# One stretch of tiled matmuls per batch over all eight PSUM banks, with four output banks and earlier loads of x

## The chip, the cores and the metric

The kernel runs on one core of a Trainium2 chip. The metric is the device time of one execution, in microseconds (us); lower is better. A kernel is run several times and the median is quoted. All runs quoted here count as undisturbed: none was more than 1.5% above the fastest run of the same kernel. Engines: PE is TensorE (matmuls), PEld its weight loads, DVE is VectorE, ACT is ScalarE, POOL is GpSimd, SP issues most of the DMAs (41 of the 53 that the page of the kernel before lists).

## The reference

The work is two layers. A cross-attention between x (8 batches, 8 heads, 512 positions, 64 wide) and a small state (32 positions per head) gives `xread` (512 rows) and `sread` (32 rows) per batch. A feed-forward layer with SiLU follows.

```
scores = 0.125 * x @ state^T;  a  = softmax(scores);   xread = a  @ state
scores2 = 0.125 * state @ x^T; a2 = softmax(scores2);  sread = a2 @ x
h = concat(xread, sread) laid out as (8 * 544 rows, 512)
out = silu(h @ w_in) @ w_out        # w_in 512 x 2048, w_out 2048 x 512
```

The kernel never forms `xread`. It multiplies state by `w_in` first (`W1 = state @ w_in`, per batch), and then `g = silu(a @ W1)`. `sread` is kept for a short ninth batch at the end.

## The kernel before: the parts that matter

Batch 0 and the start of batch 1 run in a hand-made prologue. Then come phases. **Phase k computes the output of batch k** (`g2`: four output tiles `tt` of 16 matmuls each) and, between these matmuls, does the attention and the `g` matmuls of batch k+1 (`att_tail`) and starts batch k+2 (`att_head`). The program order is fixed by hand: each engine gets its instructions in the order in which these functions are called. `fill[step]` holds what is called after output matmul number `step` (0 to 63).

The program uses eight PSUM banks, called o0, o1, w0, w1, h0, h1, a0, a1. A matmul that overwrites a bank has to wait until the bank's last contents were copied out ("evicted").

```python
def w1_m(b, j, bks):                 # a quarter of W1: 8 small matmuls, 64 x 32 tiles of the array
    for kt in range(KT):
        for half in range(2):
            nc.tensor.matmul(bank[bks[half]][ds(32 * kt, 32), :],
                sbd[ds(64 * half, 64), b, kt, half, :],
                w_in_sb[ds(64 * half, 64), kt, ds(512 * j, 512)], ...,
                tile_position=(64 * half, 32 * kt))

def w1_e(b, j, bks, engs):           # evict both banks of a quarter
    for half in range(2):
        cp(engs[half], W1[b % 2][:, half, ds(512 * j, 512)], bank[bks[half]][:])

def sread_m(b, bk): ...              # 32 small matmuls, 128 x 32 tiles
def norm_s(b, kt=0, n=4): ...        # VectorE: sums of exp, then reciprocal (n of 4 head groups)
def norm_m(b, eng, kt=0, n=4): ...   # VectorE or POOL: multiply by the reciprocal
def a_Td(b): ...                     # DMA that transposes the result into aT, which g1 reads

def g2(b, tt, ft, bk): ...           # one output matmul, 128 x 512
def o_e(b, tt, bk, eng="dve"): ...   # evict an output tile (VectorE copy), DMA it out

WP = (("w0", "w1"), ("h0", "h1"))
def W1p(b, i):                       # half of W1
    for j in range(2): w1_m(b, 2 * i + j, WP[j])
    for j in range(2): w1_e(b, 2 * i + j, WP[j], DD if j == 0 else ("act", "act"))

def phase(k, fill):
    for tt in range(4):
        bk = ("o0", "o1")[tt % 2]    # two output banks
        for ft in range(16):
            g2(k, tt, ft, bk)
            for f in fill.get(16 * tt + ft, ()): f()
        o_e(k, tt, bk)

def att_tail(fill, b, s, a0, sg, dg):
    add(fill, s, L(exs, b), L(W1p, b, 0), L(norm_s, b))          # exs: ScalarE, exp of the scores
    add(fill, s, L(norm_m, b, "dve", 0, 2), L(norm_m, b, "pool", 2, 2))
    add(fill, s, L(nc.scalar.preload_act_table, SILU))
    add(fill, s + 14, L(W1p, b, 1), L(sread_m, b, "a1"), L(sread_n, b, "a1"))
    # ... a_Td at s, sread_t at a0 + 2, sixteen g1 at sg + dg * i

for k in range(2, 7):                # the five steady phases
    fill = {}
    if k + 2 < B: load_x(k + 2, nc.sync)
    att_tail(fill, k + 1, 0, 24, 35, 1.8)
    # ... cast_xu(k + 2) at 0, att_head(k + 2) at 34 and 56
    phase(k, fill)
```

The softmax here doesn't subtract the row's maximum and nothing guards it: scores larger than these inputs give would overflow.

## Time and profile before

| | before |
|---|---|
| median time, us | 222.31 (3 runs; 222.56 with the later rounds) |
| span in the profile, us | 220.9 |
| PE busy | 210.1 us, 95% |
| granted PE clock | 1.00 in every stretch of the phases |
| a steady phase (from one phase's last output copy to the next one's) | 23.15 us (119.20 to 142.35) |

From the profile's page of the kernel before: PE's busy time, and the shares of the chain of work that ended last.

```profile
PE 210.1 (95%) x1632; PEld 103.9 (47%) x1659; DVE 83.5 (38%) x162; ACT 133.0 (60%) x219; POOL 40.8 (18%) x78
...
PE 84%; DMA 7%; ACT 3%; issue 3%; POOL 1%; DVE 1%; ACTq 0%
```

PE bounds the kernel. The next busiest engine, ScalarE, has 60%.

PE's timeline at the start of a steady phase, kernel before. Columns: start, length in us, engine, source line, operation, output and inputs, sizes, count, and in brackets any idle time ahead of it with what ended it.

```profile
96.16 0.41 PE L251 MATMUL ps_w<-w_in_sb,sbd 64*32 64x512 bf16 x8
96.39 0.56 PE L251 MATMUL ps_h<-w_in_sb,sbd 64*32 64x512 bf16 x8
97.11 2.97 PE L296 MATMUL ps_o<-w_out_sb,g 128*128 128x512 bf16 x13 [0.16 <-issue]
100.01 0.41 PE L251 MATMUL ps_w<-w_in_sb,sbd 64*32 64x512 bf16 x8
100.24 0.40 PE L251 MATMUL ps_h<-w_in_sb,sbd 64*32 64x512 bf16 x8
100.57 0.43 PE L218 MATMUL ps_a<-x_n,en 128*32 128x65 bf16 x32
101.15 2.54 PE L296 MATMUL ps_o<-w_out_sb,g 128*128 128x512 bf16 x11 [0.16 <-issue]
```

Two stretches of tiled matmuls (L251 is W1, L218 is sread) interrupt the output matmuls (L296). Full matmuls start 0.2155 us apart. The profile draws one as 0.38 us long, since they overlap. The record of the first matmul after each switch is missing, so one slot has to be added back when the gaps are measured. The two stretches then cost about 0.82 and 1.02 us.

VectorE's timeline in the next steady phase, kernel before:

```profile
119.20 0.69 DVE L79 COPY o_sb<-ps_o 128x512 f32<-128x512 f32 x1 [7.11 <-PE ps_o L296]
119.81 1.28 DVE L79 CAST W<-ps_w 128x512 bf16<-128x512 f32 x2
122.07 1.22 DVE L181 TENSOR_REDUCE rs<-en 128x32 f32<-128x1024 bf16 x1 [0.98 <-ACT en L171]
123.32 0.35 DVE L182 RECIPROCAL rs<-rs 128x32 f32<-128x32 f32 x1
123.71 0.69 DVE L186 TENSOR_TENSOR an<-en,rs 128x512 bf16<-128x512 bf16 x1
124.32 1.28 DVE L79 CAST W<-ps_w 128x512 bf16<-128x512 f32 x2
...
125.92 0.68 DVE L79 COPY o_sb<-ps_o 128x512 f32<-128x512 f32 x1
...
142.35 0.69 DVE L79 COPY o_sb<-ps_o 128x512 f32<-128x512 f32 x1 [7.11 <-PE ps_o L296]
```

The normalisation (L181, L182, L186) cannot start before exp is done on ScalarE, and the copy of the phase's first output tile (125.92) comes behind it. PE does not mind here: that bank, o0, is next written by the third tile.

From the table of waits of the kernel before (total us, times, longest):

```profile
PE ps_h L272 <- DMA aT<-an: 1.3, 1, 1.3
```

Once, in the phase from 142 us, the g matmuls waited for the transposed a.

### The profile page before, as it was taken

The page shows a single profiled execution, that of the slowest core. Times are in us where ns is not written, and L with a number is a line of the kernel's source. Part 1 is how long each engine was busy: PE and PEld are TensorE (multiplying, and loading weights), DVE is VectorE, ACT ScalarE, POOL GpSimd, SP SyncE. Part 2 cuts the span into 40 slices and gives each one's busy share as a digit, 9 for nine tenths or more (in the row PEclk, how much of TensorE's full clock was granted, in tenths as well). Part 3 has the DMA queues.
Part 4 walks back from the last instruction along what each step waited for, and adds up shares of the span by engine and source line. Part 5 has one row for each costly group of instructions (what it writes and reads, how often), then busy time and mean ns, then how long its engine had stood idle before and what let it go on. Part 6 is the DMA issues. An engine that isn't in the chain of part 4 may idle for free.

```text
span 220.9 us, 4073 instructions
## 1 busy us (share of the span) xinstructions
PE 210.1 (95%) x1632; PEld 103.9 (47%) x1659; DVE 83.5 (38%) x162; ACT 133.0 (60%) x219; POOL 40.8 (18%) x78
## 2 busy tenths in 40 slices
PE   7889999999999999999999999997999999999993
PEld 7643443443444344444444444443443444566552
DVE  4727454624920671148313841285105701111110
ACT  3754966679587937685577747781768377533210
POOL 4644722005200061004300250025000200000000
PEclk9999999999999999999999999999999999999999
DMA  5999997891251478128711863075411311111112
GB/s 189 162 258 237 182 267 94 135 286 61 86 104 50 114 218 138 55 72 232 175 48 42 218 179 88 3 227 162 90 47 47 98 47 49 49 50 47 47 50 95
DMA packets 36068, 26.52 MB, mean 120 GB/s; under 512 B 20816, under 2 KB 31312, under 8 KB 36048
## 3 DMA queue, kind: packets, MB, share of 16 engines
q1 hardware_dynamic: 28800, 19.27, 32.6%
q0 software_dynamic: 6688, 6.52, 16.2%
q10 hardware_dynamic: 560, 0.46, 0.6%
q8 instruction: 13, 0.21, 0.4%
q14 instruction: 7, 0.06, 0.1%
HBM read 17.30 MB, written 8.91 MB: 119 GB/s over the span
## 4 chain that ended last, share of the span: by engine, by line
PE 84%; DMA 7%; ACT 3%; issue 3%; POOL 1%; DVE 1%; ACTq 0%
PE ps_o L296 45%; PE ps_h L272 25%; PE ps_w L296 3%; DMA w_in_sb<-in_moe_w_in_dram 3%; PE ps_h L283 3%; DMA aT<-an 2%; PE ps_w L251 2%; DMA st_f<-in_state_dram 1%; PE ps_h L251 1%; PE ps_a L160 1%; PE ps_a L218 1%; ACT en L171 1%; PE ps_a L251 1%; ACT L171 1%; POOL an L186 1%
## 5 line engine op out<-in xcount | busy, mean ns | idle before, releaser
L296 PE MATMUL ps_o<-w_out_sb,g 128*128 128x512 bf16 x460 | 125.2, 379 | 2.5 <-issue 2.1
L280 ACT ACTIVATE g<-ps_h 128x512 bf16<-128x512 f32 x128 | 75.7, 597 | 53.2 <-PE ps_h L272 50.5
L272 PE MATMUL ps_h<-aT,W 128*128 128x512 bf16 x250 | 74.2, 379 | 2.0 <-DMA aT<-an 1.3
L296 PEld LDWEIGHTS <-g 128*128 128x128 bf16 x512 | 47.6, 98 | 51.6 <-issue 2.8
L79 DVE COPY o_sb<-ps_o 128x512 f32<-128x512 f32 x30 | 20.6, 688 | 89.9 <-PE ps_o L296 84.9
L272 PEld LDWEIGHTS <-W 128*128 128x128 bf16 x256 | 24.4, 98 | 32.4 <-DMA aT<-an 1.6
L186 POOL TENSOR_TENSOR an<-en,rs 128x512 bf16<-128x512 bf16 x7 | 10.0, 1423 | 92.7 <-ACT W L83 52.5
L81 POOL CAST x_u<-x_f 128x256 bf16<-128x256 f32 x44 | 15.5, 400 | 26.7 <-DMA x_f<-in_x_dram 24.8
L79 DVE CAST W<-ps_w 128x512 bf16<-128x512 f32 x24 | 15.4, 681 | 4.5 <-PE ps_w L251 4.5
L83 ACT ACTIVATE W<-ps_h 128x512 bf16<-128x512 f32 x24 | 13.1, 603 | 0.1
L291 ACT ACTIVATE g_s<-ps_h 128x256 bf16<-128x256 f32 x16 | 6.1, 383 | 11.2 <-PE ps_h L283 11.2
L181 DVE TENSOR_REDUCE rs<-en 128x32 f32<-128x1024 bf16 (+1 forms) x9 | 9.9, 1099 | 5.9 <-ACT en L171 5.9
L283 PE MATMUL ps_h<-xsT,w_in_sb 128*128 128x256 bf16 x64 | 9.6, 273 | 0.0
L296 PE MATMUL ps_w<-w_out_sb,g 128*128 128x512 bf16 x32 | 9.5, 379 | 0.1
L171 ACT ACT_TABLE_LOAD x7 | 9.0, 1283 | 0.1
L171 ACT ACTIVATE en<-ps_a 128x512 bf16<-128x512 f32 (+1 forms) x16 | 8.4, 568 | 0.3
L251 PEld LDWEIGHTS <-sbd 64*32 64x32 bf16 x256 | 3.2, 89 | 10.8 <-issue 10.8
L283 PEld LDWEIGHTS <-w_in_sb 128*128 128x128 bf16 x64 | 6.3, 98 | 4.1
L510 ACT ACT_TABLE_LOAD x6 | 7.7, 1283 | 0.1
L160 PEld LDWEIGHTS <-xT 128*128 128x128 bf16 x128 | 6.0, 99 | 3.5 <-DVE xT L79 0.3
L321 PE MATMUL ps_o<-zeros 128*128 128x128 bf16 (+1 forms) x48 | 6.5, 308 | 1.2 <-DVE zeros L331 1.2
L321 PEld LDWEIGHTS <-zeros 128*128 128x128 bf16 x67 | 6.1, 129 | 1.9 <-DVE zeros L331 1.2
(63 smaller groups left out, 125.9 us busy)
## 6 DMA issues: line engine op xcount, KB each, us to landing
out_dram<-o_sb SPq DMA_DIRECT2D x32, 256.0 KB, 2.4
x_f<-in_x_dram SPq DMA_DIRECT2D x5, 1024.0 KB, 6.6
w_in_sb<-in_moe_w_in_dram POOLq DMA_DIRECT2D x4, 512.0 KB, 9.6
w_out_sb<-in_moe_w_out_dram POOLq DMA_DIRECT2D x4, 512.0 KB, 9.3
x_f<-in_x_dram SPq DMA_DIRECT2D x4, 256.0 KB, 3.8
x_f<-in_x_dram POOLq DMA_DIRECT2D x2, 512.0 KB, 8.0
x_f<-in_x_dram POOLq DMA_DIRECT2D x1, 1024.0 KB, 13.0
out_dram<-o_sb ACTq DMA_DIRECT2D x1, 256.0 KB, 2.4
```

Of the source, the lines that this page charges most:

```text
L79: nc.vector.tensor_copy(dst, src)
L81: nc.gpsimd.tensor_copy(dst, src)
L83: nc.scalar.activation(dst, src, func=COPY, bias=0.0)
L171: nc.scalar.activation(en[b % 2][:, :, :, ds(kt, n), :].rearrange("p h c k s -> p k (h c) s"), v[:, ds(kt % 2, n)], func=EXP, bias=0.0, sc ...
L181: nc.vector.tensor_reduce(v, en[b % 2][:, :, :, ds(kt, n), :], axis=AX, op=ADD)
L186: e.tensor_tensor(an[b % 2][:, :, :, ds(kt, n), :].rearrange("p h c k s -> p (h c) k s"), en[b % 2][:, :, :, ds(kt, n), :].rearrange("p h ...
L251: nc.tensor.matmul(bank[bks[half]][ds(32 * kt, 32), :], sbd[ds(64 * half, 64), b, kt, half, :], w_in_sb[ds(64 * half, 64), kt, ds(512 * j, ...
L272: nc.tensor.matmul(bk[:], W1[b % 2][:, half, ds(128 * ft, 128)], aT[b % 2][:, half, :, :], start=(half == 0), stop=(half == 1), skip_group ...
L280: nc.scalar.activation(g[b % 2][:, ft, :], bk[:], func=SILU, bias=0.0)
L283: nc.tensor.matmul(bk[:, 0:256], w_in_sb[:, kt, ds(128 * ft, 128)], xsT[:, kt, :, :, :], start=(kt == 0), stop=(kt == KT - 1), skip_group_ ...
L296: nc.tensor.matmul(bank[bk][:, c0:c1], src[:, ft, ds(128 * tt, 128)], w_out_sb[:, ft, c0:c1], start=(ft == 0), stop=(ft == 15), skip_group ...
L321: nc.tensor.matmul(bank[bk][:, 0:w], zeros[:, 0:128], zeros[:, 0:w], start=True, stop=True, skip_group_check=True,)
```

## The change

Its intent is to switch the array between whole and tiled matmuls once per batch in place of twice. To hold all of W1 at once, one stretch needs all eight banks, so it stands at the border of two output tiles, the only point at which no bank holds a half-finished sum. With four output banks in rotation, the next tile's bank is not the one just finished. The normalisation is split in halves, so that POOL can start sooner. Loads of x are issued half a phase to a phase earlier.

```diff
-        WP = (("w0", "w1"), ("h0", "h1"))
-
-        def W1p(b, i):
-            for j in range(2):
-                w1_m(b, 2 * i + j, WP[j])
-            for j in range(2):
-                w1_e(b, 2 * i + j, WP[j], DD if j == 0 else ("act", "act"))
+        TB = ("o0", "w0", "o1", "w1")
+        WB = (("w1", "w0"), ("h0", "h1"), ("a0", "a1"), ("o1", "o0"))
 
         def phase(k, fill):
             for tt in range(4):
-                bk = ("o0", "o1")[tt % 2]
                 for ft in range(16):
-                    g2(k, tt, ft, bk)
+                    g2(k, tt, ft, TB[tt])
                     for f in fill.get(16 * tt + ft, ()):
                         f()
-                o_e(k, tt, bk)
+                o_e(k, tt, TB[tt])
+                for f in fill.get((tt,), ()):
+                    f()
+
+        def tiled(b):
+            for j in range(4):
+                w1_m(b, j, WB[j])
+            w1_e(b, 0, WB[0], ("act", "dve"))
+            sread_m(b, "w1")
+            for j in range(1, 4):
+                w1_e(b, j, WB[j], ("act", "dve"))
+            sread_n(b, "w1")
 
         def att_head(fill, b, s0, s1):
             ...
+            if 4 < b + 1 < B:
+                add(fill, s0, L(load_x, b + 1, nc.sync))
 
         def att_tail(fill, b, s, a0, sg, dg):
-            add(fill, s, L(exs, b), L(W1p, b, 0), L(norm_s, b))
-            add(fill, s, L(norm_m, b, "dve", 0, 2), L(norm_m, b, "pool", 2, 2))
+            add(fill, s, L(exs, b))
+            add(fill, s, L(norm_s, b, 0, 2), L(norm_m, b, "pool", 0, 2))
+            add(fill, s, L(norm_s, b, 2, 2), L(norm_m, b, "dve", 2, 2))
             add(fill, s, L(nc.scalar.preload_act_table, SILU))
-            add(fill, s + 14, L(W1p, b, 1), L(sread_m, b, "a1"), L(sread_n, b, "a1"))
+            add(fill, (0,), L(tiled, b))
             ... # sread_t reads w1 in place of a1
 
-        att_tail(fill, 2, 10, 33, 38, 1.55)          # phase 1
+        att_tail(fill, 2, 9, 33, 38, 1.55)
+        add(fill, 9, L(cast_xu, 3), L(load_x, 4, nc.sync))
             ... # phase 1: scs two steps earlier
         for k in range(2, 7):
             fill = {}
-            if k + 2 < B:
-                load_x(k + 2, nc.sync)
-            att_tail(fill, k + 1, 0, 24, 35, 1.8)
+            att_tail(fill, k + 1, 0, 28, 35, 1.8)
```

More of the change, by code (lines that the diff above doesn't have):

```diff
@@ L486 @@
         load_x(3, nc.sync)
-        WP = (("w0", "w1"), ("h0", "h1"))
-        def W1p(b, i):
-            for j in range(2):
-                w1_m(b, 2 * i + j, WP[j])
-            for j in range(2):
-                w1_e(b, 2 * i + j, WP[j], DD if j == 0 else ("act", "act"))
+        TB = ("o0", "w0", "o1", "w1")
+        WB = (("w1", "w0"), ("h0", "h1"), ("a0", "a1"), ("o1", "o0"))
         def phase(k, fill):
             for tt in range(4):
-                bk = ("o0", "o1")[tt % 2]
                 for ft in range(16):
-                    g2(k, tt, ft, bk)
+                    g2(k, tt, ft, TB[tt])
                     for f in fill.get(16 * tt + ft, ()):
                         f()
-                o_e(k, tt, bk)
+                o_e(k, tt, TB[tt])
+                for f in fill.get((tt,), ()):
+                    f()
         def add(fill, step, *fs):
-            fill.setdefault(int(step), []).extend(fs)
+            fill.setdefault(step if isinstance(step, tuple) else int(step), []).extend(fs)
         def L(f, *a):
             return lambda: f(*a)
+        def tiled(b):
[6 more added lines that the diff above has]
+            sread_n(b, "w1")
         def att_head(fill, b, s0, s1):
@@ L526, in att_tail @@
                 add(fill, s, L(a_Td, b))
-            add(fill, a0 + 2, L(sread_t, b, "a1", "dve"))
+            add(fill, a0 + 2, L(sread_t, b, "w1", "dve"))
             for i in range(16):
@@ L535 @@
         add(fill, 3, L(sread_t, 1, "a1", "dve"))
-        add(fill, 3, L(cast_xu, 3))
-        add(fill, 6, L(scs, 2, 0))
-        add(fill, 8, L(scs, 2, 1))
-        att_tail(fill, 2, 10, 33, 38, 1.55)
+        add(fill, 4, L(scs, 2, 0))
+        add(fill, 6, L(scs, 2, 1))
+        att_tail(fill, 2, 9, 33, 38, 1.55)
+        add(fill, 9, L(cast_xu, 3), L(load_x, 4, nc.sync))
         att_head(fill, 3, 37, 58)
```

## The prediction

> **What bounds it now.** TensorE (PE). The page gives PE busy 95%, and 84% of the chain of waits is PE at a granted clock of 1.00. In the timeline full matmuls (128x512) start every 0.2155 us. A steady phase (one batch, 64 output plus 32 g matmuls) lasts 23.14 us (119.00 to 142.14), of which 96 x 0.2155 = 20.7 us are those matmuls. The rest is mostly two tiled stretches. From the last normal matmul's slot to the next (the first one after each switch has no record, so I add one slot) the W1-only stretch costs about 0.82 us and the W1+sread stretch about 1.02 us: 0.1 us to enter, 0.23 us per group of eight 64x512 tiles, 0.33 us from the last group to sread, 0.37 us from sread to the next normal matmul. [...]
>
> **What the change intends.** One stretch per batch instead of two: 0.1 + 4 x 0.23 + 0.11 + 0.37, about 1.5 us instead of 1.84. That is 0.35 us saved in each of six batches, 2 us in all (0.9%). Loading x earlier takes the transfer away from the transpose of a: in one phase (142 to 167 us) PE waited 1.31 us for it, so about 1.3 us come back. Other POOL waits for x are off the chain.
>
> **What it costs.** The fourth W1 part is written to o1 and o0, and o0 is the output bank finished in the matmul just before the stretch. PE must wait for its eviction, which VectorE does in order [...], after the whole normalisation of the batch. Before, that eviction was also late (behind the normalisation), but nobody needed the bank soon.
>
> For a steady phase, from the phase's first matmul at 0: 16 outputs end their slots at 3.45, the stretch starts at 3.55, the fourth group is wanted at 4.25. ScalarE: exp table load, then first exp ends at 2.55, second at 3.04 (as now). VectorE: reduce 0.68, reciprocal 0.25, reduce 0.68, reciprocal 0.25 (the half forms of batch 0), multiply 0.69, then the copy of o0 0.69: it ends near 5.8. So PE idles about 1.6 us; the stretch ends at about 6.55, and costs 3.1 us instead of 1.84: +1.3 us in each of five phases, +6.4 us.
>
> Phase 1 is worse: exp comes only six outputs before the stretch. There, a0 and a1 wait for exp too, and o0 is free near 57.0 us, while the stretch would start near 52.3. It costs about 5.4 us against 1.96 now: +3.4 us.
>
> Sum: 6.4 + 3.4 - 1.3 = +8.5 us. The wait of sread for w1's eviction, the transposed a (issued about 1 us earlier in the phase) and W1's later evictions are in time. The tail is unchanged.
>
> **Predicted: 230.8 us; 227 to 234 holds 8 in 10. Faster by over 2%: 3%; within 2%: 11%; slower: 86%.**
>
> **What shows it.** Waits of PE: a tiled W1 matmul into ps_o, released by VectorE's o_sb copy, six times, 1.3 to 2.8 us; in phase 1 also W1 into ps_a released by exp. Steady phases of about 24.4 us instead of 23.14. The wait for aT gone. POOL's waits for x gone without gain. PE busy near 91%.
>
> **What would make it wrong.** If the copy of o0 ran before the normalisation, the stall would be nearly nil and the kernel about 1% faster. If the idle gaps lowered the granted clock (longest about 2.6 us, in phase 1), it would be slower still. If x's load now delays the transpose of x beyond its scores (10 us of slack), a new wait appears. If switching costs more than read, the gain grows.

## The result, and the profile after

| | before | after |
|---|---|---|
| median time, us | 222.56 (4 runs) | 233.52 (4 runs, 232.69 to 235.31) |
| ratio, 95% interval | | 1.0499 (1.0429 to 1.0569): slower |
| span in the profile, us | 220.9 | 231.2 |
| steady phase, us | 23.15 | 24.54 |
| mean granted clock | 1.00 | 0.991 (0.985 to 0.993 in the other runs) |

Ratios are the mean time of one kernel's runs over that of the other's of the same rounds, so they are not quite the ratios of the medians quoted.

The page, kernel after:

```profile
PE 212.3 (92%) x1633; PEld 105.1 (45%) x1659; DVE 84.3 (36%) x174; ACT 133.6 (58%) x219; POOL 39.9 (17%) x78
...
PE 80%; DVE 7%; DMA 4%; issue 4%; ACT 3%; POOL 0%; ACTq 0%
```

VectorE is less busy as a share than before (36%), and yet it has entered the chain with 7% where it had 1%. The waits of PE, kernel after:

```profile
PE ps_o L251 <- DVE o_sb L79: 9.5, 6, 2.5
...
PE ps_a L251 <- ACT en L171: 0.7, 1, 0.7
```

Six times, once per batch, a tiled W1 matmul into an output bank waits for a VectorE copy of an output tile: 9.5 us together. The wait for aT has gone. PE's timeline of a steady phase, kernel after:

```profile
101.93 3.62 PE L296 MATMUL ps_o<-w_out_sb,g 128*128 128x512 bf16 x15
105.48 0.41 PE L251 MATMUL ps_w<-w_in_sb,sbd 64*32 64x512 bf16 x8
105.71 0.40 PE L251 MATMUL ps_h<-w_in_sb,sbd 64*32 64x512 bf16 x8
105.92 0.40 PE L251 MATMUL ps_a<-w_in_sb,sbd 64*32 64x512 bf16 x8
106.14 0.38 PE L251 MATMUL ps_o<-w_in_sb,sbd 64*32 64x512 bf16 x1
107.92 0.41 PE L251 MATMUL ps_o<-w_in_sb,sbd 64*32 64x512 bf16 x7 [1.41 <-DVE o_sb L79]
108.26 0.43 PE L218 MATMUL ps_w<-x_n,en 128*32 128x65 bf16 x32
108.62 3.41 PE L296 MATMUL ps_w<-w_out_sb,g 128*128 128x512 bf16 x14
```

The fourth group of eight starts with one matmul into o1 at 106.14. The second, into o0, comes at 107.92. Without that delay of 107.92 - 106.14 = 1.78 us the stretch would take 108.62 - 105.38 - 1.78 = 1.46 us, against 0.82 + 1.02 = 1.84 us for the two before (105.38 is the next output slot, 0.1 us ahead of 105.48). So the intended saving is there, 0.38 us, and is lost under 1.78 us of standing still.

VectorE in the same phase, kernel after, shows what PE stood still for:

```profile
102.13 0.69 DVE L79 COPY o_sb<-ps_w 128x512 f32<-128x512 f32 x1 [7.11 <-PE ps_w L296]
104.52 0.69 DVE L181 TENSOR_REDUCE rs<-en 128x16 f32<-128x512 bf16 x1 [1.69 <-ACT en L171]
105.24 0.25 DVE L182 RECIPROCAL rs<-rs 128x16 f32<-128x16 f32 x1
105.41 0.63 DVE L181 TENSOR_REDUCE rs<-en 128x16 f32<-128x512 bf16 x1
106.07 0.25 DVE L182 RECIPROCAL rs<-rs 128x16 f32<-128x16 f32 x1
106.36 0.91 DVE L186 TENSOR_TENSOR an<-en,rs 128x512 bf16<-128x512 bf16 x1
107.19 0.68 DVE L79 COPY o_sb<-ps_o 128x512 f32<-128x512 f32 x1
...
126.67 0.69 DVE L79 COPY o_sb<-ps_w 128x512 f32<-128x512 f32 x1 [7.11 <-PE ps_w L296]
```

The tile in o0 was finished about 105.5. VectorE was in the middle of the normalisation, which had begun late, after exp, and copied o0 at 107.19 to 107.87. PE went on at 107.92. All of that is in order and on time for VectorE; only somebody now waits for its last item.

In phase 1 exp comes six output matmuls before the stretch, so everything is worse. PE's timeline of phase 1, kernel after:

```profile
53.50 0.90 PE L251 MATMUL ps_a<-w_in_sb,sbd 64*32 64x512 bf16 x8 [0.74 <-ACT en L171]
54.01 0.39 PE L251 MATMUL ps_o<-w_in_sb,sbd 64*32 64x512 bf16 x1
56.89 0.62 PE L251 MATMUL ps_o<-w_in_sb,sbd 64*32 64x512 bf16 x7 [2.49 <-DVE o_sb L79]
...
58.83 3.75 PE L296 MATMUL ps_w<-w_out_sb,g 128*128 128x512 bf16 x14 [0.22 <-issue]
```

And the granted clock there, kernel after. Columns: stretch, its length, PE busy (count), clock, DMA share, GB/s:

```profile
53.00:56.00 3.00, 0.78 (x9) 1.00 0.26 84
56.00:59.00 3.00, 1.90 (x41) 0.59 0.26 93
59.00:62.00 3.00, 3.00 (x13) 0.84 0.00 0
62.00:65.00 3.00, 2.81 (x21) 1.00 0.27 85
```

In windows of 0.5 us from 55 to 63 the clock reads 1.00 or 0.50, except in the two at the edges of the dip (0.55 from 56.5, 0.54 from 59.5). So (0.41 + 0.16) x 3 / 0.5 = 3.4 us passed at half clock. This began just before PE resumed, and matmuls then started 0.43 us apart.

**Where the 10.3 us of the two spans went**, from the times of each phase's last output copy: 4.7 us in all up to the end of phase 1 (73.07 before, 77.81 after), 5.6 us in the five steady phases (116.53 and 122.13 us), nothing in the tail (31.3 us in both).

### The profile page after: what moved, and what is told of

The parts are those of the page before. It is cut to its first block, busy times and chain, and to the rows that moved or that the text cites. A ratio compares the mean times of both kernels' runs of the same rounds, so it can differ in the third digit from the quotient of the medians.

```text
span 231.2 us, 4107 instructions
## 1 busy us (share of the span) xinstructions
PE 212.3 (92%) x1633; PEld 105.1 (45%) x1659; DVE 84.3 (36%) x174; ACT 133.6 (58%) x219; POOL 39.9 (17%) x78
## 3 DMA queue, kind: packets, MB, share of 16 engines
HBM read 17.30 MB, written 8.91 MB: 113 GB/s over the span
## 4 chain that ended last, share of the span: by engine, by line
PE 80%; DVE 7%; DMA 4%; issue 4%; ACT 3%; POOL 0%; ACTq 0%
PE ps_h L272 24%; PE ps_w L296 24%; PE ps_o L296 22%; DVE rs L181 3%; DMA w_in_sb<-in_moe_w_in_dram 3%; PE ps_h L283 3%; DVE o_sb L79 2%; DVE rs L182 1%; DMA st_f<-in_state_dram 1%; PE ps_a L160 1%; PE ps_o L251 1%; ACT en L171 1%; PE ps_w L218 1%; PE ps_a L251 1%; ACT L171 1%
## 5 line engine op out<-in xcount | busy, mean ns | idle before, releaser
L296 PE MATMUL ps_o<-w_out_sb,g 128*128 128x512 bf16 x248 | 69.5, 379 | 0.6 <-issue 0.2
L296 PE MATMUL ps_w<-w_out_sb,g 128*128 128x512 bf16 x243 | 68.4, 383 | 0.6 <-issue 0.2
L79 DVE COPY o_sb<-ps_w 128x512 f32<-128x512 f32 (+1 forms) x17 | 11.5, 681 | 60.0 <-PE ps_w L296 55.1
L186 POOL TENSOR_TENSOR an<-en,rs 128x512 bf16<-128x512 bf16 x7 | 7.4, 1054 | 122.4 <-ACT en L171 61.0
L79 DVE COPY o_sb<-ps_o 128x512 f32<-128x512 f32 x16 | 10.9, 686 | 36.9 <-PE ps_o L296 36.8
L81 POOL CAST x_u<-x_f 128x256 bf16<-128x256 f32 x44 | 17.8, 448 | 4.4 <-DMA x_f<-in_x_dram 4.4
L181 DVE TENSOR_REDUCE rs<-en 128x16 f32<-128x512 bf16 (+1 forms) x15 | 10.5, 697 | 15.0 <-ACT en L171 15.0
L251 PE MATMUL ps_o<-w_in_sb,sbd 64*32 64x512 bf16 x48 | 4.9, 415 | 9.5 <-DVE o_sb L79 9.5
L83 ACT ACTIVATE W<-ps_a 128x512 bf16<-128x512 f32 x13 | 7.7, 601 | 3.0 <-PE ps_a L251 3.0
L79 DVE CAST W<-ps_a 128x512 bf16<-128x512 f32 x11 | 7.5, 682 | 5.1 <-PE ps_a L251 5.1
```

What stands on the lines that cost most here:

```text
L79: nc.vector.tensor_copy(dst, src)
L81: nc.gpsimd.tensor_copy(dst, src)
L83: nc.scalar.activation(dst, src, func=COPY, bias=0.0)
L181: nc.vector.tensor_reduce(v, en[b % 2][:, :, :, ds(kt, n), :], axis=AX, op=ADD)
L186: e.tensor_tensor(an[b % 2][:, :, :, ds(kt, n), :].rearrange("p h c k s -> p (h c) k s"), en[b % 2][:, :, :, ds(kt, n), :].rearrange("p h ...
L251: nc.tensor.matmul(bank[bks[half]][ds(32 * kt, 32), :], sbd[ds(64 * half, 64), b, kt, half, :], w_in_sb[ds(64 * half, 64), kt, ds(512 * j, ...
```

## The experiments

Theory: PE waits for o0, because its copy stands behind the normalisation in VectorE's queue. Rivals: the single stretch over eight banks itself (its switches, its use of all banks) or the earlier loads of x cost the time. All kernels gave correct results. "Before" in each is a set of runs on the same chip in the same rounds (medians 222.34 to 222.56, so that medians of different rounds can be compared).

| run | what | median us | ratio to before (95%) |
|---|---|---|---|
| after | the change | 233.52 | 1.0499 (1.0429 to 1.0569) |
| e1_act_evicts | ScalarE evicts o0 | 223.67 | 1.0059 (1.0000 to 1.0118) |
| e2_mult_pool | 0.9 us less ahead of the copy | 226.33 | 1.0169 (1.0122 to 1.0215) |
| e3_extra_dve | 0.9 us more ahead of the copy | 247.83 | 1.1130 (1.1059 to 1.1201) |
| e6_phase1_old | phase 1 as before | 228.08 | 1.0240 (1.0191 to 1.0289) |
| e4_x_late | x loads as before | 233.00 | 1.0477 (1.0435 to 1.0518) |
| e5_before_x_early | before, with early x loads | 221.98 | 0.9982 (0.9948 to 1.0016) |
| e8_keep_busy | zeros in the gap of phase 1 | 231.76 | 1.0410 (1.0373 to 1.0447) |
| e7_one_later | stretch one tile later | 221.60 | 0.9963 (0.9933 to 0.9993) |
| e9_both | that, and phase 1 as before | 220.42 | 0.9923 (0.9892 to 0.9953) |

### e1_act_evicts: another engine copies o0

```diff
-                o_e(k, tt, TB[tt])
+                o_e(k, tt, TB[tt], "act" if tt == 0 and k < 7 else "dve")
-            w1_e(b, 0, WB[0], ("act", "dve"))
+            w1_e(b, 0, WB[0], ("act", "act"))
-                w1_e(b, j, WB[j], ("act", "dve"))
+                w1_e(b, j, WB[j], ("dve", "dve") if j == 1 else ("act", "dve"))
-            add(fill, s, L(nc.scalar.preload_act_table, SILU))
-            add(fill, (0,), L(tiled, b))
+            add(fill, (0,), L(tiled, b), L(nc.scalar.preload_act_table, SILU))
```

The first W1 quarter had to move as well: the next output tile is written to w0, whose copy would else have been the next to stand behind the normalisation.

> The changed kernel, but ScalarE evicts the first output tile of a phase (o0) and both banks of the first W1 part, VectorE both banks of the second, and ScalarE loads the SILU table after these. Theory (the fourth W1 part waits for o0, whose copy stands behind the normalisation in VectorE's order): ScalarE is free when the tile ends, so o0 is free about 4.3 us into a steady phase when it is wanted at 4.2; PE's wait for it falls from 1.4 us to about 0.1, a steady phase from 24.5 us to about 23.2; in phase 1 the wait falls from 2.5 to about 0.6 and the clock does not dip. About 223 us in all (221.5 to 224.5). Rival (the one stretch of eight banks itself, its mode switches or the early x loads cost the time): stays near 233.

Measured: 223.67 us, within its range. The wait for o0 is no longer in the table of waits, a steady phase takes 23.17 us (100.28 to 123.45), and phase 1 keeps its full clock (the profiled run's mean of 0.989 comes from a dip in the prologue, after PE had waited 1.83 us for a load of weights). The single stretch and the early loads are still in it, so they are not what cost 11 us. The intended saving does not appear in this run: its stretch takes 105.41 - 103.53 = 1.88 us and not 1.46, because PE now waits briefly for ScalarE, which copies o0, w1 and w0 one behind the other (the last copy ends at 105.36).

### e2_mult_pool and e3_extra_dve: shorten and lengthen VectorE's queue

```diff
 e2: -            add(fill, s, L(norm_s, b, 2, 2), L(norm_m, b, "dve", 2, 2))
     +            add(fill, s, L(norm_s, b, 2, 2), L(norm_m, b, "pool", 2, 2))
 e3: -            add(fill, s, L(norm_s, b, 2, 2), L(norm_m, b, "dve", 2, 2))
     +            add(fill, s, L(norm_s, b, 2, 2), L(norm_m, b, "dve", 2, 2), L(norm_s, b, 2, 2))
```

> The changed kernel, but the second half of the normalisation's multiply goes to POOL as well, which takes 0.91 us out of VectorE's queue ahead of the copy of o0, and nothing else. Theory: the wait of PE for o0 falls by about 0.83 us in each of six phases (1.4 to about 0.6), total about 228.5 us; up to 1.5 us less if the clock no longer dips in phase 1. Rival: VectorE's queue is not what PE waits for: 233 as before, or later because POOL delays the transpose of a.

> The changed kernel, but the second half's reduce and reciprocal are done twice, the second time behind the multiply, so that about 0.9 us more stands ahead of the copy of o0 in VectorE's queue (results unchanged). VectorE is busy 36% of the span, so by its load alone nothing would change. Theory: each of six waits grows by about 0.9 us, total about 239 us (238 to 242, with a longer dip of the clock). Rival: 233 to 234.

The waits of PE for o0, in e2 and then in e3:

```profile
PE ps_o L251 <- DVE o_sb L79: 3.6, 6, 1.5
```

```profile
PE ps_o L251 <- DVE o_sb L79: 15.2, 6, 3.4
```

From 9.5 us in the changed kernel they went to 3.6 and 15.2: about 1 us per wait either way. e2 lost 7.2 us of time, 5.9 of it waits; its profiled run kept its clock, so that part of the rest is the dip. Its expected value, 228.5 (up to 1.5 less), was too high by 0.7 us or more.

e3 missed its expected 239 by nearly 9 us, on the slow side. The waits grew as expected (5.7 us); the rest is the clock, 0.952 on average. After each of the six gaps of 2.1 us and more the page shows it low. One of them, a steady phase of e3, by windows:

```profile
84.00:87.00 3.00, 1.02 (x26) 1.00 0.02 5
87.00:90.00 3.00, 2.61 (x44) 0.66 0.67 170
90.00:93.00 3.00, 3.00 (x13) 0.77 0.00 0
93.00:96.00 3.00, 3.00 (x17) 1.00 0.36 100
```

With the same arithmetic, (0.34 + 0.23) x 3 / 0.5 = 3.4 us at half clock, here after a gap of 2.14 us. Over the whole span, (1 - 0.952) x 247.3 / 0.5 = 23.7 us passed at half clock, seven times 3.4 (twice in phase 1, where the clock reads 0.50 from 58 to 64 us; the windows of the other four phases give 3.4 us each as well), where the change has it once. So six more dips go with 14.3 - 5.7 = 8.6 us beyond the waits, about 1.4 us each. A longer dip had been expected for phase 1 only.

### e6_phase1_old: phase 1 alone undone

Phase 1 got back its two stretches (functions `W1p` and the old `att_tail`) and two output banks; the five steady phases are those of the change. Its load of x for batch 4 stayed in phase 1.

> The changed kernel with phase 1 alone as in the kernel before (two stretches, two output banks). Theory: phase 1 costs 5.0 us more than before, 3.4 of it waits and about 1.6 the half clock that follows them; both go: about 228.5 us, granted clock 1.00. Rival (the five steady phases' own waits of 1.4 us also lower the clock, or phase 1 costs no more than one steady phase): a clock below 1.00, or about 232.

Measured: 228.08 us, clock 1.00 (0.997 to 1.00 over its four runs). Of the loss of 11.0 us, 5.4 are phase 1's and its clock's. The five waits left add up to 6.7 us, the longest 1.4, and no dip follows any of them.

### e4_x_late and e5_before_x_early: the loads of x

e4 is the change with the loads where they were; e5 is the kernel before with the loads moved as the change moves them:

```diff
 e5:         def att_head(fill, b, s0, s1):
                 ...
     +            if 4 < b + 1 < B:
     +                add(fill, s0, L(load_x, b + 1, nc.sync))
             ...
     +        add(fill, 10, L(load_x, 4, nc.sync))      # phase 1
     -            if k + 2 < B:
     -                load_x(k + 2, nc.sync)
```

> The changed kernel with the loads of x where the kernel before had them, at the start of a phase. Theory: the early loads cost nothing on PE's chain except that POOL's cast of x, no longer late, runs beside VectorE's multiply, which took 0.91 us in place of 0.69; without it PE's waits for o0 shrink by about 0.2 us in five phases: about 232.5 us (231.5 to 234). The transpose of a has 2.9 us of slack after the stall, so it causes no wait. Rival (moving the loads is what made the kernel slow): 223 to 226.

> The kernel before with the loads of x alone moved one phase ahead. Theory: the one wait of PE for the transposed a (1.3 us) goes, nothing else on the chain changes: about 221.2 us, ratio 0.994 (0.990 to 0.998). Rival (the wait came from the transpose itself and not from x's load beside it): ratio 1.000.

e4: 233.00 us, within its range; the loads are not the loss. But the reason for which it expected 1 us less was wrong: PE's wait for o0 is 9.5 us in e4 too, and VectorE's multiply still takes 0.91 us, although POOL's cast of x now comes more than 3 us later. The cast did not slow it. One more thing is in this run: PE's wait for the transposed a is absent, although the loads are late and the slowest transposition took 5.1 us.

e5: 221.98 us, ratio 0.9982, not told apart from 1, where 0.994 was expected. Its waits show why:

```profile
PE ps_h L272 <- DMA aT<-an: 1.3, 1, 1.3
```

The one wait for the transposed a is still there, in the same phase and of the same length, with no load of x beside it. One transposition of the five lands after 4.8 us in the kernel before, in e5 and in the change alike (median 3.0 to 3.1). It is not the load of x that makes that one slow. What does stays open: a packet on the instruction queue q8 falls into that window and not into the same window of the phase before, but no run tests that.

### e8_keep_busy: does the gap cause the half clock?

```diff
         def tiled(b):
             for j in range(4):
+                if j == 3 and b == 2:
+                    warm(10, "o1", 512)      # ten matmuls of zeros into a bank that is free here
                 w1_m(b, j, WB[j])
```

> The changed kernel with ten matmuls of zeros (2.2 us at full clock) put where PE idles in phase 1, before the fourth W1 part, into a bank that is free there; results unchanged. Theory: the half clock after the gap follows from the gap of 2.5 us; kept busy, PE keeps its clock: granted clock 1.00 and about 1.6 us less, 231.9 us (231 to 232.8), in all runs alike. Rival (the clock falls for something else, or the zeros do not count as activity): about 233.5 or more, clock 0.985 to 0.993.

Measured: 231.76 us, within its range. The clock over the same windows, e8:

```profile
53.00:56.00 3.00, 2.14 (x29) 1.00 0.46 150
56.00:59.00 3.00, 3.00 (x50) 1.00 0.22 83
```

PE has to wait as long as before (in both kernels the copy of o0 ends 4.70 us after the stretch's first matmul), but does something meanwhile, and the half clock is gone (1.00 in three of four runs, 0.998 in one). The medians differ by 233.52 - 231.76 = 1.8 us. In the profiled runs, from the first W1 matmul of phase 1 to the first matmul of the third output tile, it is 62.42 - 52.13 = 10.29 us in the change and 61.67 - 52.76 = 8.91 us here, 1.4 us less. The gap causes the dip. One dip costs 1.4 us by the profiled runs; the 1.8 us of the medians also holds two runs of the change that, by their mean clock, had more than one.

### e7_one_later and e9_both: the stretch where VectorE is free

```diff
 e7:
-        WB = (("w1", "w0"), ("h0", "h1"), ("a0", "a1"), ("o1", "o0"))
+        WB = (("w1", "o1"), ("h0", "h1"), ("a0", "a1"), ("o0", "w0"))
-            add(fill, (0,), L(tiled, b))
+            add(fill, (1,), L(tiled, b))
-            att_tail(fill, k + 1, 0, 28, 35, 1.8)
+            att_tail(fill, k + 1, 0, 40, 41, 1.4)
     ... # att_head at 37 and 58; in phase 1 a0 = 40, g matmuls from 44 every 1.19 steps
 e9: e7 with phase 1 as in e6, and
-            att_tail(fill, k + 1, 0, 40, 41, 1.4)
+            att_tail(fill, k + 1, 0, 40, 36, 1.75)
     ... # att_head at 37 and 57
```

After the second tile the normalisation is over. The bank just finished is now w0, so w0 comes last. The bank of the next tile, o1, comes first, so that it is copied out in time.

> The changed kernel with the one stretch after the second output tile of a phase in place of the first, when the normalisation is long done; the last W1 part waits for w0, the bank just finished, the first one takes the bank of the next tile; g matmuls start at step 41 (44 in phase 1). Theory: VectorE is free when the tile ends, PE's wait for the bank is about 0.2 us, a steady phase about 22.9 us against 23.14 before, no dip of the clock; with the wait for the transposed a gone too about 220 us in all, ratio to before 0.989 (0.983 to 0.995). Rival (a single stretch over eight banks costs what it saves in switches): 222 or more. A new wait for ScalarE at the closer g matmuls would show at the h banks.

> Phase 1 as in the kernel before; in the five steady phases one stretch after the second output tile, as in the run one_later, but with g matmuls from step 36 every 1.75 outputs in place of from 41 every 1.4. Theory: phase 1 gives back the 1.3 us it cost in that run, the g matmuls no longer crowd ScalarE (0.1 us per phase); steady phases 22.95 us; no wait for the transposed a, since it is issued long before its use: about 220.3 us, ratio 0.990 (0.986 to 0.995). Rival: no version of the single stretch gains, ratio 0.996 or more.

e7: 221.60 us, ratio 0.9963 (0.9933 to 0.9993): by the 2% rule the same as before, a little faster if anything, and above its range (0.983 to 0.995). The steady phase is 23.04 us where 22.9 was expected, and phase 1 still waits: for o0 (0.5 us), for w0 (0.2), and 0.4 us each for the multiply and for ScalarE's copy of the transposed a (0.2 in the kernel before). e9 undid phase 1 and spread the g matmuls wider, two changes at once: 220.42 us, ratio 0.9923 (0.9892 to 0.9953), in its range, and a steady phase of 22.95 us as expected. VectorE in a steady phase of e9:

```profile
99.47 0.91 DVE L186 TENSOR_TENSOR an<-en,rs 128x512 bf16<-128x512 bf16 x1
100.30 0.68 DVE L79 COPY o_sb<-ps_o 128x512 f32<-128x512 f32 x1
102.16 0.69 DVE L79 COPY o_sb<-ps_w 128x512 f32<-128x512 f32 x1 [1.18 <-PE ps_w L296]
```

VectorE now waits for PE (1.18 us ahead of the copy of w0). PE still waits for w0, but only 0.19 us of a stretch (102.71 to 102.90), which is half of the 0.38 us saved. e9 is 0.8% faster than the kernel before. That is less than the 2% that a verdict asks for, but its interval lies clear of 1. No kernel here beat it.

Where does this gain come from? In the profiled runs the five steady phases of e9 differ from those before: four are shorter, by 0.03, 0.20, 0.20 and 1.68 us, and the last is 0.12 us longer, which makes 1.99 us. The 1.68 us belong to the phase in which the kernel before waited 1.3 us for the transposed a, and that wait is absent in e9. So most of the gain is this wait, and the other four phases together give only 0.3 us. In e9 a's transposition is issued 5.28 us into a phase (100.53 - 95.25), in the kernel before 6.15 us (102.20 - 96.05), while its first use comes about as late (9.44 and 9.53 us). The split of the normalisation is the likely reason. Whether that split alone would bring the same gain with the two stretches kept, no run tests.

## Why the prediction was right, point by point

- **Direction and size.** 230.8 us was predicted (227 to 234) and 233.52 measured, near the upper end. Slower by over 2% was given 86%. A loss of 8.5 us was forecast and 11.0 measured; phase 1 holds 1.3 us of the difference and the steady phases, taken together, 0.5 (5.6 in place of 6.4 - 1.3). The rest is mostly the difference between the medians and the profiled runs (11.0 and 10.3 us).
- **The cause** was named: the fourth W1 part waits for o0, whose copy stands behind the normalisation in VectorE's order. The waits show it, six times. e1 removes it, e2 and e3 scale it. The order was taken from the program and the durations from the trace of the kernel before. The trace of the change shows VectorE keeping that order: o0 is finished about 105.5, but its copy starts only at 107.19, as the multiply (106.36 to 107.27) ends.
- **The intended saving.** About 1.5 us for the single stretch was predicted, and 1.46 us is left after subtracting the wait. The gain of one stretch less is 0.38 us; no run separates the parts of a switch.
- **Steady phases.** +1.3 us each was predicted. Measured: +1.34, +1.39, +1.64 and +1.36 us in the four that had no wait for aT before. The multiply took 0.91 us and not the 0.69 assumed. VectorE's multiply took 0.91 us where POOL's had started 0.70 us earlier (kernel after, 106.36 and 105.66) and 0.69 us where it started first (kernel before, 123.71 and 123.81); POOL's took 1.05 us in the first case and 1.50 in the second. That would fit two multiplies that slow each other, but no run isolates it.
- **Phase 1.** +3.4 us was predicted and about 4.7 measured. The term that was mis-sized is the clock: "if the idle gaps lowered the granted clock (longest about 2.6 us, in phase 1), it would be slower still" stood under what would make it wrong, and counted as zero in the sum. It happened: e8 prices it at 1.4 us. In the traces of the change and of e3 the clock in a dip is 0.50, for about 3.4 us, and for twice that in phase 1 of e3. Two of the four runs of the change had a mean clock of 0.985, which by the same arithmetic is (1 - 0.985) x 232 / 0.5 = 7 us at half clock, about two dips. They are the two slowest of the four (234.03 and 235.31).
- **The step that failed:** "Loading x earlier takes the transfer away from the transpose of a [...] so about 1.3 us come back." The wait did go in the changed kernel, but not for this reason. With the loads alone moved (e5) it stays at 1.3 us, and with all of the change but the loads (e4) it is absent. What the change gives instead is room. In the changed kernel the transposition is issued at 107.42 and first used at 113.06, 5.6 us later, where the kernel before had 102.20 to 105.58, 3.4 us. Measured from the phase's start (the last output copy of the phase before), the issue is 0.9 us earlier, as the prediction also noted, and PE, held up by o0, comes 1.4 us later. So even the slow transposition of 4.8 us is in time. A right number came from a wrong cause, which is luck; only the runs with that part alone (e5) and without it (e4) showed it.

## What to carry to other kernels

When a change makes an engine wait for a buffer sooner than before, look at what stands ahead of the buffer's release in the *queue* of the engine that frees it. Its busy share says nothing: VectorE was idle 64% of the span and still cost 9.5 us. Moving the consumer to where that queue is empty took away the loss of 5% (e7: ratio 0.9963), and with phase 1 undone as well (e9) a gain of 0.8% was left, most of it from a wait for a DMA and not from the saved switch. A PE gap should be priced with the half clock that may follow it (here, in the phases, after gaps of 2.14 us and more, 1.4 us a dip). And a single part of a change should be run alone before a gain is put down to it.

## What stays open

- How long a gap of PE brings half clock. Gaps of 2.14 us (e3) and 2.49 us (the change, 0.9 us of matmuls after another gap of 0.74 us) did. After waits for o0 of up to 1.65 us no dip followed in the profiled runs. In the prologue one followed a wait of 1.83 us (e1) and none a wait of 1.9 us (e5), so the border is not sharp.
- What a switch of the array is made of. 0.1 us passed on entering the tiled mode, and one stretch less saved 0.38 us per batch.
- Why one of five equal DMA transpositions landed after 4.8 us in place of 3.0. The load of x is excluded by e5.
